# Moving weight decoding from a feed forward into the attention before it, two more PSUM banks at the start, and a later set of first splits

## The chip, the cores and the metric

The kernel runs on one core of a Trainium2 chip. The metric is the device time of one execution in microseconds (us). A measured change is compared with the kernel before on the same chip.

## The reference

```python
scores = scale * np.matmul(q, k.transpose(0, 1, 3, 2))      # 4 batches, 12 heads, 448 x 64
scores = np.einsum('bhij,hg->bgij', scores, w_pre)          # heads mixed
attn = softmax(scores)
attn = np.einsum('bhij,hg->bgij', attn, w_post)             # heads mixed again
x = np.matmul(attn, v)                                      # -> 1792 tokens x 768
h = x @ w_in                                                # 768 x 2048
x = (h / (1 + np.exp(-1.702 * h))) @ w_out                  # 2048 x 768
# then a mixture of 8 experts, one per token by argmax(x @ w_gate):
out[mask] = gate_w * eom * (np.maximum(x[mask] @ w1[e], 0) @ w2[e])
```

Everything is computed to float32 accuracy. `w_in` and `w_out` arrive as 64-bit floats.

## The kernel before

The program has three parts, each an unrolled list of instructions in an order written out by hand. Each engine runs its own instructions strictly in that order, and so does SP, which issues nearly all transfers.

**The attention** (`attention`) has 92 steps `s`, each of up to 20 query rows for all heads: four batches of 23 steps, in tiles of 120 rows. Scores are made by `qk` for a tile `t` of 112 queries (four to a batch) and one of six pairs of heads `p`, emptied from PSUM by `qk_ev` (one half on ScalarE, L166, one on VectorE, L167) into `so`, and sent to a DRAM tensor `S`. `relay(s)`, issued three steps ahead, reads them back as `G`, with heads on partitions. In step s TensorE does `premix(s)` (L184), VectorE the row maximum (L188), ScalarE the exponential (L191); `weights(s-1)` makes reciprocals on VectorE (L194, L195) and from them on GpSimd the matrices `M` (L198); `post(s-2)` multiplies by them (L207); `av` multiplies by V (L225). Before the loop stands an outset: scores of the first two tiles from unsplit q and k (`raw=True`), 12 pairs, two PSUM banks each, of which the pool `pq` has two.

**Split operands.** A float32 operand of later matmuls is split in a rounded part (a cast on ScalarE) and a rest (a subtraction on VectorE or GpSimd); three matmuls make one product. `split_w` (L317, L318) does so for a half of the feed forward's weights, `split_x` (L309, L310) for a chunk of its input.

**Decoding** (`Words`). The 32 halves of `w_in` and `w_out`, 128 x 768 each, come as 64-bit words. One half is decoded by four instructions on VectorE (L72 to L75) and an Abs on ScalarE (L67). The first NE halves are decoded one instruction at a time during the attention, in every other step from step 10 on, and lie in `pre`; the others are decoded in the first batch of the feed forward by `upto`, into `res`. `pre` also has two raw buffers behind the decoded halves.

**The feed forward** (`moe1`) has 64 steps, 16 for each of four batches: `l1` (18 matmuls, L326), tanh and product (`act`, L331, L332), split of the result (`act2`, L335, L336), `l2` (18 matmuls, L343). Its beginning is laid into the last steps of the attention: from step 88 on each step asks twice for the next of `EARLY`'s items. An item (t, kind, arguments) runs once the t-th request has been made; 'x' is `split_x`, 'w' `split_w`, 'l' `l1`, 't' `act`, 'u' `act2`; 'v' puts the subtraction on VectorE, 'p' on GpSimd.

**The experts** (`moe2`) follow. Their weights come through a ring of NR + NP buffers, NP in `pre`, NR in `res`; gathered tokens lie in `pre` behind the first NP.

Of the kernel before, what the change touches and what calls it, by code (L numbers as in the profile page):

```python
# [6 lines left out]
F32 = mybir.dt.float32  # L7
# [9 lines left out]
B, H, S, D = 4, 12, 448, 64  # L17

TI, TQ = 120, 112
TILES = [(i, min(TI, S - i)) for i in range(0, S, TI)]  # L20
DM, FF, E = 768, 2048, 8
# [3 lines left out]
CHUNK = {256: 128, 288: 96, 318: 106}  # L25
CM, CP, SL = max(CAP), 96, 1920

NE, NR, NP = 9, 12, 3

EARLY = [(2,'x',(2,'p')),(2,'x',(0,'v')),(3,'w',(0,0,'p')),(3,'x',(1,'v')),(4,'x',(5,'p')),(4,'x',(4,'v')),(5,'x',(3,'p')),  # L30
    (5,'w',(1,0,'p')),(6,'l',(0,)),(7,'w',(0,1,'v')),(8,'l',(1,)),(9,'w',(2,0,'p')),(9,'t',(0,)),(10,'u',(0,)),(11,'l',(2,)),(12,'w',(1,1,'v'))]
BIG = 2.0 ** 20


# [59 lines left out]
                    if k==2: self.after(i)  # L94
            self.nd=h[-1]+1

def attention(tc, qT, kT, vT, w_pre, w_post, x_out, words, beside=None):


    nc=tc.nc  # L100
    tiles=[(b,i0,n) for b in range(B) for i0,n in TILES]; NB=S//TQ
# [26 lines left out]
            sel(out=y,in_=y,pattern=[[0,12],[12,5]],compare_op=ALU.is_ge,fill=0.0,base=11,channel_multiplier=-1)  # L128
    R={}; K={}; V={}; Q={}; St={}; G={}; PM={}; E={}; ST={}; M2={}; PA={}; AT={}; PV={}; QP={}; WA={}; ready=set(); moved=set()
    def dma_k(b,p,n=2):  # L130
        if p%2==0: R['k',b,p//2]=wf.tile([128,2,S],F32,tag="kr",bufs=3,name="kr")
        nc.sync.dma_start(out=R['k',b,p//2][:,p%2:p%2+n],in_=kT[b,2*p:2*p+2*n].rearrange("(p h) d s -> (h d) p s",h=2))
    def split(k,d,x,shape,bufs,n=None):

# [17 lines left out]
        nc.sync.dma_start(out=R['q',t][:,lo:hi],in_=qT[b,:,6*TQ*j+lo:6*TQ*j+hi])  # L152
    def qk(t,p,raw=False):
        b=t//NB; i=slice(p*TQ,p*TQ+TQ)
        for z in range(2): QP[t,p,z]=pq.tile([TQ,S],F32,tag="q",name="psq")
        if raw: pairs=((R['q',t],R['k',b,p//2]),)
        else: (qh,ql),(kh,kl)=Q[t,],K[b,p//2]; pairs=((qh,kh),(qh,kl),(ql,kh))
        for x,(q,k) in enumerate(pairs):
            for z in range(2):
                r=slice(64*z,64*z+64)  # L160
                nc.tensor.matmul(QP[t,p,z],q[r,i],k[r,p%2],start=x==0,stop=x==len(pairs)-1)  # L161
# [8 lines left out]
    def relay(s):  # L170
        t,k,n=steps[s]; b,i0,_=tiles[t]; k+=i0
        if (b*NB+(k+n-1)//TQ,5) not in moved: raise RuntimeError('relay before scores')
        G[s]=w.tile([124,2,S],F32,tag="G",bufs=6,name="G")
        x=St[b].rearrange("i h j -> (i h) j")
        for a in units(s):
            if qs(s,a,1)==5: nc.sync.dma_start(out=G[s][64*a:64*a+60],in_=x[12*(k+10*a):12*(k+10*a)+120].rearrange("(c p) j -> p c j",c=2))
            else:
                for c in range(2): nc.sync.dma_start(out=G[s][64*a:64*a+12*qs(s,a,c),c],in_=x[12*(k+10*a+5*c):12*(k+10*a+5*c+qs(s,a,c))])
# [46 lines left out]
            for z in range(2): nc.tensor.matmul(ps[64*z:64*z+64,p%3,:n],V[b,2*p+z][:,j,:],AT[t][:,j,2*p+z,:n],start=j==0,stop=j==3)  # L225
    def av_ev(t,p):
        if p%3<2: return
        b,i0,n=tiles[t]; x=w.tile([128,3*TI],F32,tag="X",bufs=3,name="X")[:,:3*n]
        nc.vector.tensor_copy(x.rearrange("d (p i) -> d p i",p=3),PV.pop((t,p//3))[:,:,:n])  # L229
        nc.sync.dma_start(out=x_out[b,:,6*i0+(p-2)*n:6*i0+(p+1)*n],in_=x)  # L230
    from collections import defaultdict
    at={k:defaultdict(list) for k in 'qakvdKD'}
# [8 lines left out]
    for t in range(NT):  # L241
        b=tiles[t][0]
        m=first[t+2]-first[t+1] if t+1<NT else 3
        for p in range(6): at['a'][first[t+1]+2+p*m//6].append((t,p))
        if t%4==0:
            for h in (0,3,6,9): at['v'][first[t]+(h//3 if t==0 else (0,4,5,7)[h//3])].append((b,h))

    dma_q(0,(0,2*TQ)); dma_k(0,0,1); dma_k(0,1,1); dma_q(0,(2*TQ,6*TQ)); dma_k(0,2); dma_k(0,4)
    dma_q(1)
# [6 lines left out]
    for s in range(0,NS+6):  # L256
        on=s<NS
        if s+LEAD<NS: relay(s+LEAD)
        for x in at['d'][s]: dma_q(*x)
        for x in at['k'][s]: dma_k(*x)  # L260
        for x in at['v'][s]: dma_v(*x)
        if on:
            premix(s)
            for a in units(s): maxi(s,a); exp(s,a)
        if 0<=s-2<NS:
            for a in units(s-2): post(s-2,a)
            for c in range(2): post_ev(s-2,c)
        if 0<=s-1<NS: weights(s-1)
        for x in at['a'][s]: av(*x); av_ev(*x)
        if words is not None and s>7 and s%2==0 and next(words,"end")=="end": words=None  # L270
        for x in at['q'][s]: qk(*x)
        for x in at['q'][s]: qk_ev(*x)
        for x in at['K'][s]: split_k(*x)
        for x in at['D'][s]: split_q(*x)
        if s+LEAD>=NS-1 and beside is not None:
            if front is not None: front.close(); front=None
            for _ in range(2):
                if beside is not None and beside()=="end": beside=None
# [5 lines left out]
def moe1(tc, env, x_in, D, wg):  # L284

    nc=env.nc; NF=FF//128
    with ExitStack() as ctx, ExitStack() as late:
# [110 lines left out]
        at=0; did=set()  # L398
# [14 lines left out]
        for s in range(NS):  # L413
            b,f=steps[s]
            if s+1<NS and ('t',s+1) not in did: act(s+1)
            if s+2<NS and ('w',s+2,0) not in did: split_w(s+2,0)
            if b>0 and f==0: evac(b-1)
            if s+1<NS and ('u',s+1) not in did: act2(s+1)
            if s+1<NS and ('w',s+1,1) not in did: split_w(s+1,1)

            D.upto(NE+7*(s+1)//4)
            if b==3 and f>8:
                for i in range((f-9)*2,(f-8)*2 if f<NF-1 else NR+NP): env.load_w(i)
            nb_=b+1
            if s+2<NS and ('l',s+2) not in did: l1(s+2)
            if nb_<4 and f==NF-3:
                if b==0: split_w(16,0); did.add(('w',16,0))
                for c in range(6): split_x(nb_,c)
            if s==14: split_g()
            if b==0 and f<13: env.setup[f]()  # L430
            if f==3 and b<3: load_x(b+1)
            if b>0 and f in QS: route(b-1,(0,1,2,4,3)[QS.index(f)])
            if b==3 and f==8: rank(0)
            if b==3 and f==9: first(0)
            if b>0 and f in RS: i=RS.index(f); rows(b-1,i//2,i%2)
            if b>0 and f==1:
                def between(i):
                    if i==0: lsplit(b-1,0)
                    if i<5: lsplit(b-1,i+1)
                    lmm(b-1,i)  # L440
                l2(s,between)
            elif b>0 and f==2: l2(s,lambda i: lfin(b-1) if i==1 else None)
            elif s==NS-1:

                def between(i):
                    if i>0: evac(3,((2,3,4,5,0,1)[i-1],))
                    do(LR[i])
                def do(a):
                    for x in a:
                        if x[0]=='L': logits(3,(2,3,4,5,0,1)[x[1]],x[1]==0,x[1]==5)  # L450
                        elif x[0]=='R': route(3,x[1])
                        elif x[0]=='F': first(x[1])
                        else: rows(3,x[1],x[2])
                l2(s,between)
                between(6)
                do(LR[7])
            else: l2(s)
# [196 lines left out]
def moe2(tc, env, out):  # L654

    nc=env.nc
    with ExitStack() as ctx:
# [12 lines left out]
        def load_x(e):  # L670
            C,CP,NC=CS[e]
            if e==0: ID[e],ig=env.id0,env.ig0
            else:
                ID[e]=p.tile([128,3,4],I32,tag="id",bufs=3,name="id")[:CP,:NC,:]
                i=nc.sync.dma_start(out=ID[e],in_=env.ids[0:E*SL,:].rearrange("(e s) o -> e s o",e=E)[bass.ds(env.expert(e),1),0:C,:].rearrange("x (c p) o -> (x p) c o",p=CP))
                env.after(i.ins,'a')
                ig=p.tile([128,3],I32,tag="ig",bufs=2,name="ig")[:CP,:NC]
                nc.vector.tensor_scalar_min(ig,ID[e][:,:,0],float(NTOK-1))
            IG[e]=ig
            XS[e]=env.pre[:,(7+3*(e%2))*DM:(10+3*(e%2))*DM].rearrange("p (c n) -> p c n",c=3)[:CP,:NC,:]  # L680
            for c in range(NC):
                nc.gpsimd.indirect_dma_start(out=XS[e][:,c,:],out_offset=None,in_=env.rows,in_offset=IOA(ap=ig[:,c:c+1],axis=0))
        def load_g(e):
# [152 lines left out]
def moe_kernel(tc, qT, kT, vT, w_pre, w_post, w_in, w_out, wg, wm, out):  # L836
    with ExitStack() as ctx:
        x=ctx.enter_context(tc.tile_pool(name="xd",bufs=1,space=bass.MemoryType.DRAM)).tile([B,128,6*S],F32,name="x_dram")
        with tc.manual_schedule():
            pre=ctx.enter_context(tc.tile_pool(name="pre",bufs=1)).tile([128,(NE+4)*DM],F32,name="pre")  # L840
            D=Words(tc.nc,pre,w_in,w_out)
            def rest():
                env=make_env(tc,ctx,tc.nc); env.wm=wm; env.pre=pre
                yield from moe1(tc,env,x,D,wg)
                yield env
            g=rest()
            attention(tc,qT,kT,vT,w_pre,w_post,x,D.early(),lambda: next(g))
            env=None
            while not isinstance(env,Env): env=next(g)
            moe2(tc,env,out)  # L850
            env.stack.close()
        overflow(tc,env,out)
# [48 lines left out]
```

## Time and profile before

| | |
|---|---|
| median of 3 runs | 1306.34 us (1304.58 to 1307.55) |
| profiled execution | 1307.6 us, its span 1305.9 us |
| mean granted TensorE clock | 0.972 |
| TensorE busy | 1191.5 us (91%) |
| VectorE busy | 784.1 us (60%) |
| ScalarE busy | 613.4 us (47%) |
| GpSimd busy | 297.3 us (23%) |
| transfers | 201.12 MB |

Times in the profile run from the start of the span. PE is TensorE's matmuls, PEld its weight loads, DVE VectorE, ACT ScalarE, POOL GpSimd, SP the engine that issues transfers; L12 is line 12 of the kernel before. A busy share is an average over stages with different limits, so it is read stage by stage. "Idle before" is the time an engine stood still ahead of an instruction, with what ended it.

### The profile page before, as it was taken

The page shows a single profiled execution, that of the slowest core. Times are in us where ns is not written, and L with a number is a line of the kernel's source. Part 1 is how long each engine was busy: PE and PEld are TensorE (multiplying, and loading weights), DVE is VectorE, ACT ScalarE, POOL GpSimd, SP SyncE. Part 2 cuts the span into 40 slices and gives each one's busy share as a digit, 9 for nine tenths or more (in the row PEclk, how much of TensorE's full clock was granted, in tenths as well). Part 3 has the DMA queues.
Part 4 walks back from the last instruction along what each step waited for, and adds up shares of the span by engine and source line. Part 5 has one row for each costly group of instructions (what it writes and reads, how often), then busy time and mean ns, then how long its engine had stood idle before and what let it go on. Part 6 is the DMA issues. An engine that isn't in the chain of part 4 may idle for free. (4 is left out here: it accounts for less than half of the span.)

```text
span 1305.9 us, 32101 instructions
## 1 busy us (share of the span) xinstructions
PE 1191.5 (91%) x13254; PEld 1010.5 (77%) x13255; DVE 784.1 (60%) x1403; ACT 613.4 (47%) x1215; POOL 297.3 (23%) x366
## 2 busy tenths in 40 slices
PE   7788888889999888899999999999969799999996
PEld 2365656556666677788999899989969799999996
DVE  1576777667776499985435443545346555666662
ACT  2564665556555344444335433443325344444452
POOL 0442353344322400001211121112121230321110
PEclk9898999989989899999999999999989999999998
DMA  6897998888886146401000100001655754656400
GB/s 215 264 306 228 286 295 256 282 241 261 275 256 189 49 174 219 145 26 43 12 22 11 43 23 13 9 1 52 242 197 176 216 169 144 221 194 217 144 20 22
DMA packets 101715, 201.12 MB, mean 154 GB/s; under 512 B 30143, under 2 KB 72261, under 8 KB 101564
## 3 DMA queue, kind: packets, MB, share of 16 engines
q1 hardware_dynamic: 95484, 186.84, 45.5%
q0 software_dynamic: 6080, 12.18, 2.9%
q8 instruction: 106, 1.74, 0.6%
q14 instruction: 45, 0.37, 0.1%
HBM read 143.60 MB, written 56.43 MB: 153 GB/s over the span
## 5 line engine op out<-in xcount | busy, mean ns | idle before, releaser
L326 PE MATMUL psh<-x,ws 128*128 128x448 f32 x1152 | 250.9, 370 | 16.5 <-DVE ws L318 16.5
L343 PE MATMUL pso<-g,ws 128*128 128x448 f32 x1152 | 252.9, 370 | 0.0
L326 PEld LDWEIGHTS psh<-x,ws 128*128 128x128 f32 x1152 | 216.7, 189 | 40.6 <-DVE ws L318 20.2
L343 PEld LDWEIGHTS pso<-g,ws 128*128 128x128 f32 x1152 | 213.6, 188 | 20.3
L207 PEld LDWEIGHTS psa<-M,E 60*64 60x64 f32 x5760 | 107.5, 138 | 93.9 <-issue 51.8
L191 ACT ACTIVATE E<-psm,st 124x448 f32<-124x448 f32 x180 | 112.5, 630 | 101.9 <-DVE st L188 101.8
L318 DVE TENSOR_TENSOR ws<-res,ws 128x768 fp32r<-128x768 f32 x92 | 99.9, 1086 | 90.1 <-ACT ws L317 86.8
L198 POOL TENSOR_SCALAR M<-wq,st 124x60 f32<-124x60 f32 x180 | 99.8, 571 | 237.0 <-DVE st L195 226.6
L702 PE MATMUL psh<-xt,ws 128*128 128x256 f32 (+2 forms) x1152 | 149.4, 290 | 3.4 <-DVE hh L706 3.4
L336 POOL TENSOR_TENSOR g<-th,g 128x448 fp32r<-128x448 f32 x49 | 56.6, 1155 | 420.2 <-ACT g L335 419.6
L207 PE MATMUL psa<-M,E 60*64 60x60 f32 x5760 | 113.8, 223 | 42.1 <-issue 30.6
L702 PEld LDWEIGHTS psh<-xt,ws 128*128 128x128 f32 x1152 | 146.4, 191 | 4.2 <-DVE hh L706 4.0
L188 DVE TENSOR_REDUCE st<-psm 124x1 f32<-124x448 f32 x180 | 104.2, 618 | 30.9 <-PE psm L184 30.4
L669 DVE TENSOR_TENSOR ws<-res,ws 128x768 fp32r<-128x768 f32 x98 | 93.5, 959 | 30.1 <-ACT ws L668 27.0
L721 PE MATMUL psy<-ws,hh 128*128 128x384 f32 x576 | 110.9, 346 | 0.0
L335 ACT CAST g<-th 128x448 fp32r<-128x448 f32 x64 | 36.3, 567 | 144.0 <-PE pso L343 102.6
L721 PEld LDWEIGHTS psy<-ws,hh 128*128 128x128 f32 x576 | 101.4, 191 | 0.0
L184 PE MATMUL psm<-G,wp 60*64 60x448 f32 x720 | 97.5, 585 | 2.2 <-DMA G<-S 1.4
L167 DVE TENSOR_SCALAR so<-psq 112x448 f32<-112x448 f32 x96 | 59.8, 623 | 61.8 <-PE psq L161 54.5
L225 PE MATMUL psv<-AT,V 128*64 128x120 f32 (+1 forms) x1536 | 95.3, 269 | 0.5 <-DVE X L229 0.5
L215 DVE COPY AT<-psa 128x480 f32<-128x480 f32 (+1 forms) x92 | 61.6, 670 | 41.9 <-PE psa L207 41.5
L166 ACT ACTIVATE so<-psq 112x448 f32<-112x448 f32 x96 | 52.2, 543 | 69.1 <-PE psq L161 45.4
(190 smaller groups left out, 1513.0 us busy)
## 6 DMA issues: line engine op xcount, KB each, us to landing
S<-so SPq DMA_DIRECT2D x96, 392.0 KB
G<-S SPq DMA_DIRECT2D x176, 210.0 KB
res<-in_wm SPq DMA_DIRECT2D x43, 768.0 KB
pre<-in_wm SPq DMA_DIRECT2D x13, 768.0 KB
pre<-in_w_in SPq DMA_DIRECT2D x11, 768.0 KB
pre<-in_w_out SPq DMA_DIRECT2D x11, 768.0 KB
V<-in_vT SPq DMA_DIRECT2D x16, 384.0 KB
qr<-in_qT SPq DMA_DIRECT2D x15, 336.0 KB
```

Of the source, the lines that this page charges most:

```text
L184: nc.tensor.matmul(PM[s,a][64*c:64*c+64],wp[r],G[s][r,c,:],start=True,stop=True)
L188: nc.vector.reduce_max(ST[s][:,0,a:a+1],PM[s,a][:124],axis=AX.X,negate=True)
L191: nc.scalar.activation(E[s,a],PM.pop((s,a))[:124],AF.Exp,bias=ST[s][:,0,a:a+1],scale=1.0,accum_out=ST[s][:,1,a:a+1])
L198: nc.gpsimd.tensor_scalar_mul(M2[s,a],wq,st[:,3,a:a+1])
L207: nc.tensor.matmul(PA[s][64*cp:64*cp+64,c,240*a+60*cc:240*a+60*cc+60],e[r,j:j+64],m[r],start=True,stop=True)
L225: for z in range(2): nc.tensor.matmul(ps[64*z:64*z+64,p%3,:n],V[b,2*p+z][:,j,:],AT[t][:,j,2*p+z,:n],start=j==0,stop=j==3)
L318: (e or nc.vector).tensor_tensor(out=t[:,1,:],in0=r,in1=t[:,0,:].bitcast(F32),op=ALU.subtract)
L326: nc.tensor.matmul(ps[:,:TB],t[:,wz,c],x[:,xz,:],start=k==0,stop=k==17); k+=1
L343: nc.tensor.matmul(OB[b][o][:,:TB],t[:,wz,c],g[:,xz,:],start=f==0 and k==0,stop=f==NF-1 and k==2)
L669: nc.vector.tensor_tensor(out=t[:,1,:],in0=r[:,c],in1=t[:,0,:].bitcast(F32),op=ALU.subtract)
L702: nc.tensor.matmul(ps,w[:,a,k*128:(k+1)*128],x[:,b,:],start=k==0 and (a,b)==(0,0),stop=k==5 and a==1)
L721: nc.tensor.matmul(PY[e][2*c+z],h[:,a,c*CP:c*CP+CP],w[:,b,z*384:z*384+384],start=f==0 and k==0,stop=f==7 and k==2)
```

## The change

Seven edits come together.

- NE goes from 9 to 13, NR from 12 to 10, NP from 3 to 5: four more halves are decoded during the attention and kept in `pre`, `res` is two rows shorter, and the ring of the experts keeps its 15 buffers. The places in `pre` follow.
- Decoding in the attention starts one step later and advances in two steps of three. In the feed forward it advances by 7 halves in 5 steps, where it was 7 in 4.
- The raw K of the first batch lies in the free end of `pre` (`spare`). `kr` has two buffers for three, `G` five for six, `X` two for three.
- Raw scores of every odd pair of heads take their two banks from `pm`, the pool of `premix`, which has three.
- The four loads of V of the first batch are issued in steps 3 to 6, where it was 0 to 3.
- EARLY's items run two requests, one step, later.
- All of EARLY's splits are on VectorE; six were on GpSimd.

```diff
-NE, NR, NP = 9, 12, 3
-
-EARLY = [(2,'x',(2,'p')),(2,'x',(0,'v')),(3,'w',(0,0,'p')),(3,'x',(1,'v')),(4,'x',(5,'p')),(4,'x',(4,'v')),(5,'x',(3,'p')),
-    (5,'w',(1,0,'p')),(6,'l',(0,)),(7,'w',(0,1,'v')),(8,'l',(1,)),(9,'w',(2,0,'p')),(9,'t',(0,)),(10,'u',(0,)),(11,'l',(2,)),(12,'w',(1,1,'v'))]
+NE, NR, NP = 13, 10, 5
+
+EARLY = [(4,'x',(2,'v')),(4,'x',(0,'v')),(5,'w',(0,0,'v')),(5,'x',(1,'v')),(6,'x',(5,'v')),(6,'x',(4,'v')),(7,'x',(3,'v')),
+    (7,'w',(1,0,'v')),(8,'l',(0,)),(9,'w',(0,1,'v')),(10,'l',(1,)),(11,'w',(2,0,'v')),(11,'t',(0,)),(12,'u',(0,)),(13,'l',(2,)),(14,'w',(1,1,'v'))]
...
     def dma_k(b,p,n=2):
-        if p%2==0: R['k',b,p//2]=wf.tile([128,2,S],F32,tag="kr",bufs=3,name="kr")
+
+        if p%2==0: R['k',b,p//2]=spare[:,p*S:p*S+2*S].rearrange("d (p j) -> d p j",p=2) if b==0 else wf.tile([128,2,S],F32,tag="kr",bufs=2,name="kr")
...
     def qk(t,p,raw=False):
-        for z in range(2): QP[t,p,z]=pq.tile([TQ,S],F32,tag="q",name="psq")
+
+        for z in range(2): QP[t,p,z]=pm.tile([128,S],F32,tag="m",name="psq")[:TQ] if raw and p%2 else pq.tile([TQ,S],F32,tag="q",name="psq")
...
     def relay(s):
-        G[s]=w.tile([124,2,S],F32,tag="G",bufs=6,name="G")
+        G[s]=w.tile([124,2,S],F32,tag="G",bufs=5,name="G")
...
     def av_ev(t,p):
-        b,i0,n=tiles[t]; x=w.tile([128,3*TI],F32,tag="X",bufs=3,name="X")[:,:3*n]
+        b,i0,n=tiles[t]; x=w.tile([128,3*TI],F32,tag="X",bufs=2,name="X")[:,:3*n]
...
-            for h in (0,3,6,9): at['v'][first[t]+(h//3 if t==0 else (0,4,5,7)[h//3])].append((b,h))
+            for h in (0,3,6,9): at['v'][first[t]+(3+h//3 if t==0 else (0,4,5,7)[h//3])].append((b,h))
...
-        if words is not None and s>7 and s%2==0 and next(words,"end")=="end": words=None
+        if words is not None and s>7 and s%3<2 and next(words,"end")=="end": words=None
...
-            D.upto(NE+7*(s+1)//4)
+            D.upto(NE+7*(s+1)//5)
...
-            XS[e]=env.pre[:,(7+3*(e%2))*DM:(10+3*(e%2))*DM]
+            XS[e]=env.pre[:,(2*NP+1+3*(e%2))*DM:(2*NP+4+3*(e%2))*DM]
...
-            attention(tc,qT,kT,vT,w_pre,w_post,x,D.early(),lambda: next(g))
+            attention(tc,qT,kT,vT,w_pre,w_post,x,D.early(),pre[:,NE*DM:],lambda: next(g))
```

## Rows read from the trace of the kernel before

**Rows 1.** Busy time by stretch: PE, PEld, DVE, ACT, POOL, granted clock, DMA share, GB/s.

```profile
460.00:576.00 116.00, 99.49 (x466) 87.71 (x465) 109.60 (x146) 54.45 (x82) 0.60 (x3) 0.99 0.46 157
576.00:700.00 124.00, 124.00 (x624) 112.39 (x624) 61.83 (x96) 53.51 (x94) 22.09 (x19) 1.00 0.09 23
50.00:430.00 380.00, 333.75 (x8166) 231.42 (x8158) 274.95 (x599) 224.41 (x539) 138.28 (x197) 0.97 0.85 262
```

**Rows 2.** Groups by line, 460 to 575 us: busy us, mean ns | idle before, releaser.

```profile
L326 PEld LDWEIGHTS psh<-x,ws 128*128 128x128 f32 x234 | 44.4, 193 | 24.3 <-DVE ws L318 20.2 <-ACT ws L317 0.4
L318 DVE TENSOR_TENSOR ws<-res,ws 128x768 fp32r<-128x768 f32 x22 | 21.0, 956 | 0.5
L75 DVE SCALAR_TENSOR_TENSOR res<-wa,res 128x768 f32<-128x768 f32 x22 | 20.2, 954 | 0.4
...
L336 DVE TENSOR_TENSOR g<-th,g 128x448 fp32r<-128x448 f32 x13 | 8.1, 622 | 4.9 <-ACT g L335 4.9
...
L72 DVE TENSOR_SCALAR res<-res 128x768 int32<-128x768 int32 x10 | 5.5, 554 | 0.0
```

**Rows 3.** Timeline of PE from 576 us: start us, us, what.

```profile
577.84 3.90 PE L326 MATMUL psh<-x,ws 128*128 128x448 f32 x18
...
592.52 3.81 PE L326 MATMUL psh<-x,ws 128*128 128x448 f32 x18
```

**Rows 4.** Timeline at the end of the attention, 404 to 478 us.

```profile
427.70 3.33 DVE L310 TENSOR_TENSOR x<-xs,x 128x448 fp32r<-128x448 f32 x2 [4.50 <-ACT x L309]
...
428.48 2.08 POOL L318 TENSOR_TENSOR ws<-pre,ws 128x768 fp32r<-128x768 f32 x1
...
433.65 1.83 PEld L207 LDWEIGHTS psa<-M,E 60*64 60x64 f32 x64 [6.71 <-POOL M L198]
...
457.36 3.98 PE L343 MATMUL pso<-g,ws 128*128 128x448 f32 x18
```

**Rows 5.** Timeline at the outset, 0 to 46 us.

```profile
6.75 1.84 PE L161 MATMUL psq<-kr,qr 64*112 64x448 f32 x4 [0.72 <-DVE so L167]
...
9.21 1.96 PE L161 MATMUL psq<-kr,qr 64*112 64x448 f32 x4 [0.63 <-ACT so L166]
...
31.29 0.62 DVE L167 TENSOR_SCALAR so<-psq 112x448 f32<-112x448 f32 x1 [3.81 <-DMA S<-so]
...
33.89 0.62 DVE L167 TENSOR_SCALAR so<-psq 112x448 f32<-112x448 f32 x1 [1.98 <-PE psq L161]
...
44.73 0.51 DVE L139 CAST Qh<-qr 128x672 fp32r<-128x672 f32 x1 [5.44 <-DMA qr<-in_qT]
```

**Rows 6.** Timeline of POOL, steps with and without a decode.

```profile
90.91 1.36 POOL L198 TENSOR_SCALAR M<-wq,st 124x60 f32<-124x60 f32 x2 [2.45 <-DVE st L195]
94.68 0.83 POOL L198 TENSOR_SCALAR M<-wq,st 124x60 f32<-124x60 f32 x2 [2.42 <-DVE st L195]
```

**Rows 7.** Waits, 82 to 396 us: us in total, times, longest.

```profile
PE psa L207 <- issue: 26.7, 18, 3.5
PEld psa L207 <- POOL M L198: 24.6, 49, 2.2
```

**Rows 8.** Queues, transfer sizes; two stretches of 25 us, and PE's waits in one.

```profile
q8 instruction: 106, 1.74, 0.6%
...
S<-so SPq DMA_DIRECT2D x96, 392.0 KB
...
pre<-in_w_in SPq DMA_DIRECT2D x11, 768.0 KB
...
250.00:275.00 25.00, 16.80 (x430) 12.08 (x432) 13.36 (x31) 12.53 (x29) 8.64 (x10) 0.98 1.00 320
...
325.00:350.00 25.00, 24.37 (x600) 17.78 (x592) 19.26 (x44) 14.89 (x37) 8.04 (x12) 1.00 0.86 264
...
PE psa L207 <- issue: 8.8, 3, 3.5
```

**Rows 9.** Busy time by stretch at the outset.

```profile
4.00:8.00 4.00, 3.09 (x8) 0.94 (x8) 0.62 (x1) 0.54 (x1) 0.00 (x0) 1.00 0.97 303
```

More of the change, by code (lines that the diff above doesn't have):

```diff
@@ L95, in upto, with attention @@
             self.nd=h[-1]+1
-def attention(tc, qT, kT, vT, w_pre, w_post, x_out, words, beside=None):
+def attention(tc, qT, kT, vT, w_pre, w_post, x_out, words, spare, beside=None):
     nc=tc.nc
@@ L679, in load_x @@
             IG[e]=ig
-            XS[e]=env.pre[:,(7+3*(e%2))*DM:(10+3*(e%2))*DM].rearrange("p (c n) -> p c n",c=3)[:CP,:NC,:]
+            XS[e]=env.pre[:,(2*NP+1+3*(e%2))*DM:(2*NP+4+3*(e%2))*DM].rearrange("p (c n) -> p c n",c=3)[:CP,:NC,:]
             for c in range(NC):
```

## The prediction, made before the result was known

> **What bounds the kernel now.** I read the table of busy time over stretches first, because the average over the span mixes stages with different limits. Three stretches matter [rows 1]. In the attention (50 to 430 us) TensorE is busy 334 of 380 us, VectorE 275, and the transfers take 0.85 of their engines: nothing is full, and everything waits a little for everything. In the first batch of the first feed forward (460 to 576) VectorE is busy 109.6 of 116 us and TensorE 99.5. From 576 TensorE is busy without a gap, so whatever an earlier stage saves reaches the end one for one.
>
> The groups by line, inside 460 to 575, say what the feed forward waits for [rows 2]: TensorE's weight loads stood idle 24.3 us, 20.2 of them for the splits of L318, and L318 itself hardly waited (0.5 us). So VectorE sets the pace here, and much of its work is the decoding of L72 to L75. How fast TensorE could go shows right behind: with no decode left, two steps of 36 matmuls each go from 577.84 to 592.52 [rows 3], 7.34 us a step. From the first `l2` at 457.36 [rows 4] to 577.84 there are 13.5 such steps (that `l2`, then `l1` and `l2` of 13 steps): 99 us of work in 120.5 us. The stretch can give back 21 us at most.
>
> Last the timeline of the two places at which the diff puts things elsewhere. At the end of the attention VectorE stood at L310, waiting 4.50 us for a cast and then running two splits in 3.33 us while GpSimd did a split of its own; the row maxima had to come behind it, and TensorE's weight loads sat idle 6.71 us until 433.65 [rows 4]. At the outset one pair of score matmuls takes 1.84 us, then both banks must be emptied, and the next pair starts 2.46 us after it; the evictions of the second tile end in the same rhythm (31.29, 33.89), the first of these held up 3.81 us by a store [rows 5].
>
> **The change part by part**, against the profiled execution (span 1305.9, time 1307.6 us, 1.3 above the median of the runs).
>
> *Four halves leave the feed forward.* 23 halves were decoded there, 19 remain. One half is one L72 (0.554 us) and three of L73 to L75 (0.954 us each) [rows 2]: 3.42 us, four of them 13.7 us. In the stretch VectorE is 0.945 busy [rows 1], so nearly all of it can show. Left are 19 x 3.42 + 14 x (two L318 at 0.956, the split of `g` at 0.622 and the tanh product, taken as long: 3.16) = 109 us by summed durations, against 123 before; scaled to the 120.5 us of the stretch, 107. TensorE needs 99, so the two become nearly equal, and as the decodes come by one or two halves a step, some of the unevenness will stay. I take -11, two short of that; ends -8 (unevenness costs 40 per cent) and -13.7 (all of it).
>
> *The same four halves enter the attention*, 16 instructions of VectorE more, two steps of three instead of one of two. (In steps 81 to 87 there were none.) VectorE has room, so the price is delay, not work: behind a two-input decode the two `M` products of GpSimd took 1.36 us, without 0.83 [rows 6], so TensorE's next `post` gets its operand 0.53 later. TensorE's loads waited for `M` 49 times in the 70 or so steps from 82 to 396 [rows 7], that is in 0.7 of them. 12 two-input decodes x 0.53 x 0.7 = 4.5, and 0.5 for the four others and for four more Abs on ScalarE (224 of 380 us busy [rows 1], so mostly covered): +5. Ends: 0 (steps without a decode take it back) and +15 (16 x 0.95, were VectorE on the chain throughout).
>
> What two engines do to each other here has a rule in the Trainium skill, "SBUF — State Buffer", section "SBUF: two separate sides": a VectorE instruction with two SBUF inputs and a GpSimd one exclude each other, and the later waits for the whole of the earlier. The trace agrees (0.53 is less than the 0.95 of a decode: it had begun before). What the rule allows at its worst, a decode that begins just ahead of each `M`, is among the rivals below.
>
> *Weights moved with them*: 4 x 768 KB [rows 8] = 3.1 MB more during the attention, some 10 us of the transfer engines at the 320 GB/s of the stretch from 250 to 275 [rows 8]. TensorE's "issue" idle at L207 was 8.8 us in that stretch (share 1.00), and it was busy 16.8 of 25 us there, but 24.4 in 325 to 350 (0.86) [rows 8]; TensorE's program itself comes by a queue of 106 packets, 1.74 MB [rows 8], so I read these waits as instructions arriving late, an inference. 10 us of full transfer engines are 0.4 such stretches: 0.4 x 8.8 = 3.5 at worst; nearer the middle, +1.7, ends 0 and +5. The Trainium skill, "Runtime: NRT & Kernel Launch", section "Instruction fetch mechanics", calls the cost of a block boundary mostly hidden. By that this term would be 0 and the sum 1.7 less; the 8.8 us speak against it.
>
> *The tail.* The splits of EARLY come one step later and all on VectorE. The wait for the cast (4.50 us [rows 4]) goes, because the transfer has landed by then, and so does the doubling of durations: splits of `x` without a GpSimd split beside them should take what that of `g`, of the same shape, takes (0.62 [rows 2]). The first stall of 6 us shrinks to perhaps 0.5. Late next are `post` and the first `l1`, one step later and so no longer a filler in front of `post(90)`: an estimate from the order of the work, 1.5 us of new idle time there. -6 + 0.5 + 1.5 = -4; ends -1 and -6.
>
> *The outset.* With two more banks TensorE need not wait for the eviction: 1.84 for 2.46, 0.62 x 5 gaps = -3.1 in the first tile. The second hangs on stores and on three buffers of `so`: VectorE waited 3.81 us for a store [rows 5]. That chain moves up by the same 3.1, and its last two gaps shrink to 1.84 too: -1.2. Sum -4.3. Ends: -1 (the transfer engines are at 0.97 from 4 to 8 us [rows 9], so that the stores, not the banks, may limit) and -7 (gaps at 1.3, what a store of 392 KB [rows 8] takes at the 303 GB/s of that row: 7 gaps x 1.15 = 8, less one for the loads that still run).
>
> *Moved and shortened.* The four loads of V leave steps 0 to 3, where the first `Qh` waited 5.44 us for its transfer [rows 5], and go to steps 3 to 6, among the stores and G loads: 0, ends -1.5 and +2 (one load is 1.3 us at the same rate). With two buffers of `kr` the third K load of a batch now waits on SP for `split_k` of the next step, and stores and G loads queue behind it for about a step (380 us are some 91 steps, 4.2 each [rows 1]). G is loaded three steps ahead, which hides it: +0.5, ends 0 and +4. G with five buffers and X with two: nothing, since four G live at once and an X is sent a tile (six steps) before its buffer returns. NR, NP and the place of `XS` shift names; halves lie under the same turn of `load_w`: 0.
>
> Sum: -11 + 5 + 1.7 - 4 - 4.3 + 0 + 0.5 = -12.1 on 1307.6, or 1295.5; less the 1.3 that the profile lies above the median, 1294.2. I say **1294**.
>
> **Rivals.**
> *The attention hides the decodes* (0 instead of +5) and the outset gives its 7: 1294 - 5 - 2.7 = 1286. For it: VectorE is idle 28% there. Against: 49 waits for `M`.
> *GpSimd held for whole decodes, and TensorE soon the bound*: were each of the 12 two-input decodes to hold `M` for its full 0.95 us, they would cost 11, and the feed forward gives 8: 1294 + 6 + 3 = 1303, hardly to be told from now. The rule quoted from the Trainium skill ("SBUF — State Buffer", the same section) would allow it. For it: 49 waits of 70; against: 1.36 is what a pair took behind a decode.
> *Slower*: full transfer engines starve TensorE's program. The issue waits of L207, 26.7 us from 82 to 396 [rows 7], are worst where the share is 1.00, and the change adds bytes there and moves the loop up against the same bytes. Were they to grow by 20 us (1.3 us in each of fifteen stretches of 25 us), 1294 - 1.7 + 20 = 1312. From 14 us on, the gain is gone. Against: only 3% more bytes (3.1 MB on 262 GB/s x 380 us [rows 1], 100 MB).
> *The banks do nothing*, since the stores limit: 4.3 less gain, 1298; that is inside the forecast's own range.
>
> **How the numbers follow.** What this kernel's measurement can tell from no change is 0.2%, 2.6 us: faster is below 1303.7, slower above 1309. Forecast 0.62 (1289 to 1300 by its own ends), hidden 0.14, held 0.12, slower 0.12. Of the forecast and the first rival all is faster (0.76), of the held rival a third (0.04), the rest of it mostly the same: faster 0.80, same 0.08, slower 0.12. The range leaves out the slower rival and half of the hidden one's low side: 1284 to 1305.
>
> **What would show it.** Right: between the first `l2` and the first gapless stretch some 109.5 us instead of 120.5, with VectorE still above 0.9; the first `l2` about 1 us earlier than 457.36; L310 near 0.6 us, no idle of 6 us at L207 in the tail; pairs at the outset under 2 us apart, and a first `Qh` near 40. Wrong: an attention longer by more than 5 us once outset and tail are taken out, more issue idle at L207, or SP waiting for a K split while TensorE waits for G. The prediction fails most easily in the attention, where a price of 5 is set between 0 and 15.

## The result, and the profile after

The changed kernel takes 1312.67 us (median of 20 runs, 1302.84 to 1323.79), the kernel before 1306.51 (20 runs). The ratio is 1.0059 (95% interval 1.0040 to 1.0078): slower by 0.6%, 7.7 us, where 1294 was forecast. The two medians by themselves are 6.2 us apart; the ratio leaves out the longest run of the changed kernel, a slow one, and the text goes by it. The profiled execution took 1314.0 us, span 1312.3, mean granted clock 0.959 (0.972 before).

Line numbers are those of each run's own kernel: L168, L169 and L209 of the changed one are L166, L167 and L207 of the kernel before.

The stages first, from four marks in the timeline of each trace: the first cast to `Qh`, the last `premix`, the first `l2`, the first `l1` of the second batch.

| us | to first `Qh` | attention | tail | feed forward, first batch | rest |
|---|---|---|---|---|---|
| before | 44.73 | 382.02 | 30.61 | 120.48 | 728.1 |
| after | 38.73 | 399.16 | 29.59 | 120.47 | 724.3 |

The outset gained 6.0 us, the attention lost 17.1. The feed forward, at which the largest term was aimed, did not move.

Busy time by stretch after (columns as in [rows 1]); the first row is the feed forward's first batch, the second the attention:

```profile
467.00:588.00 121.00, 107.26 (x503) 95.99 (x498) 103.51 (x137) 53.89 (x81) 3.07 (x22) 0.94 0.38 126
...
50.00:430.00 380.00, 328.59 (x7759) 227.49 (x7754) 278.81 (x591) 216.69 (x518) 138.41 (x187) 0.95 0.83 261
```

And the same stretch of the feed forward in the kernel before:

```profile
457.00:578.00 121.00, 104.49 (x499) 92.08 (x495) 113.30 (x152) 57.06 (x85) 3.08 (x22) 0.99 0.45 152
```

VectorE does 9.8 us less in the feed forward (103.5 for 113.3; its term said 13.7), and yet the 121 us stay. TensorE's idle time fell by 2.8 us only (16.5 to 13.7), and its matmuls took 2.8 longer (104.5 to 107.3) at a lower granted clock (0.94 for 0.99). In the attention TensorE does less in the same 380 us (328.6 for 333.8), with the transfers no fuller.

What SP waited for in the attention of the changed kernel, 40 to 430 us (us in total, times, longest), and then what the engines waited for, 46 to 420 us, columns as in [rows 7]:

```profile
SPq L170 <- DVE so L169: 80.2, 53, 7.3
...
SPq L133 <- POOL Kl L141: 23.0, 3, 9.2
```

```profile
PE psa L209 <- issue: 23.0, 17, 3.0
...
ACT so L168 <- DMA S<-so: 19.0, 5, 9.5
...
DVE so L169 <- DMA S<-so: 17.7, 4, 8.8
PEld psq L163 <- ACT so L168: 14.9, 9, 5.9
```

L133 is the K load, L141 the split that frees its buffer: three waits of 23.0 us in all, one for each later batch; in the kernel before, that wait is 0.4 us. The evictions of scores then waited 19.0 and 17.7 us for score stores to empty a `so`, and TensorE for the evictions. The kernel before has a single row of that kind in the same stretch:

```profile
ACT so L166 <- DMA S<-so: 2.3, 2, 1.2
```

The `issue` wait of the slower rival is not larger than before (30.6 us there in the same stretch).

The outset after, VectorE's timeline, answers to [rows 5]:

```profile
18.94 0.62 DVE L169 TENSOR_SCALAR so<-psq 112x448 f32<-112x448 f32 x1 [0.76 <-DMA S<-so]
27.84 0.62 DVE L169 TENSOR_SCALAR so<-psq 112x448 f32<-112x448 f32 x1 [8.27 <-DMA S<-so]
28.77 0.63 DVE L169 TENSOR_SCALAR so<-psq 112x448 f32<-112x448 f32 x1 [0.31 <-DMA S<-so]
30.29 0.62 DVE L169 TENSOR_SCALAR so<-psq 112x448 f32<-112x448 f32 x1 [0.89 <-PE psq L163]
...
38.73 0.51 DVE L140 CAST Qh<-qr 128x672 fp32r<-128x672 f32 x1 [5.59 <-DMA qr<-in_qT]
```

The tail after, VectorE's and the weight loads' timelines, answers to [rows 4]:

```profile
440.52 1.16 DVE L312 TENSOR_TENSOR x<-xs,x 128x448 fp32r<-128x448 f32 x2 [1.91 <-ACT x L311]
```

```profile
438.87 1.27 PEld L209 LDWEIGHTS psa<-M,E 60*64 60x64 f32 x64 [0.79 <-POOL M L200]
...
445.27 1.80 PEld L209 LDWEIGHTS psa<-M,E 60*64 60x64 f32 x64 [4.25 <-POOL M L200]
```

The stall of 6.71 us is down to 0.79, and one of 4.25 stands a `post` later.

### The profile page after: what moved, and what is told of

It reads as the page before. It is cut to its first block, busy times and chain, and to the rows that moved or that the text cites. A ratio compares the mean times of both kernels' runs of the same rounds, so it can differ in the third digit from the quotient of the medians.

```text
span 1312.3 us, 32112 instructions
## 1 busy us (share of the span) xinstructions
PE 1195.2 (91%) x13254; PEld 1018.6 (78%) x13255; DVE 788.0 (60%) x1409; ACT 612.9 (47%) x1215; POOL 295.6 (23%) x360
## 3 DMA queue, kind: packets, MB, share of 16 engines
q8 instruction: 106, 1.74, 0.6%
## 5 line engine op out<-in xcount | busy, mean ns | idle before, releaser
L328 PE MATMUL psh<-x,ws 128*128 128x448 f32 x1152 | 254.2, 374 | 13.7 <-DVE ws L320 12.5
L328 PEld LDWEIGHTS psh<-x,ws 128*128 128x128 f32 x1152 | 220.7, 192 | 37.1 <-DVE ws L320 14.8
L209 PEld LDWEIGHTS psa<-M,E 60*64 60x64 f32 x5760 | 110.5, 142 | 88.8 <-issue 44.8
L200 POOL TENSOR_SCALAR M<-wq,st 124x60 f32<-124x60 f32 x180 | 105.7, 603 | 249.2 <-DVE st L197 237.7
L209 PE MATMUL psa<-M,E 60*64 60x60 f32 x5760 | 118.0, 228 | 34.6 <-issue 23.0
L320 DVE TENSOR_TENSOR ws<-res,ws 128x768 fp32r<-128x768 f32 x76 | 82.7, 1088 | 76.8 <-ACT ws L319 73.3
L186 PE MATMUL psm<-G,wp 60*64 60x448 f32 x720 | 102.1, 600 | 1.1 <-DMA G<-S 0.8
L169 DVE TENSOR_SCALAR so<-psq 112x448 f32<-112x448 f32 x96 | 59.7, 622 | 69.1 <-PE psq L163 33.8
L227 PE MATMUL psv<-AT,V 128*64 128x120 f32 (+1 forms) x1536 | 98.2, 274 | 2.0 <-issue 1.4
L671 DVE TENSOR_TENSOR ws<-res,ws 128x768 fp32r<-128x768 f32 x80 | 76.3, 959 | 24.3 <-ACT ws L670 21.7
L168 ACT ACTIVATE so<-psq 112x448 f32<-112x448 f32 x96 | 52.1, 543 | 79.1 <-DMA S<-so 31.5
L227 PEld LDWEIGHTS psv<-AT,V 128*64 128x64 f32 x1536 | 78.4, 142 | 8.8 <-issue 2.3
```

The costliest lines, as they stand in the source:

```text
L186: nc.tensor.matmul(PM[s,a][64*c:64*c+64],wp[r],G[s][r,c,:],start=True,stop=True)
L200: nc.gpsimd.tensor_scalar_mul(M2[s,a],wq,st[:,3,a:a+1])
L209: nc.tensor.matmul(PA[s][64*cp:64*cp+64,c,240*a+60*cc:240*a+60*cc+60],e[r,j:j+64],m[r],start=True,stop=True)
L320: (e or nc.vector).tensor_tensor(out=t[:,1,:],in0=r,in1=t[:,0,:].bitcast(F32),op=ALU.subtract)
L328: nc.tensor.matmul(ps[:,:TB],t[:,wz,c],x[:,xz,:],start=k==0,stop=k==17); k+=1
L671: nc.vector.tensor_tensor(out=t[:,1,:],in0=r[:,c],in1=t[:,0,:].bitcast(F32),op=ALU.subtract)
```

## The experiments

Two theories of the loss were set against each other. *K wait*: SP issues strictly in order, so a K load that waits for its buffer holds everything behind it. *Decodes*: the four halves, with their weights and the fuller transfers, slow the attention. For the feed forward: VectorE's work is less but comes in bunches, against the rival that something else sets the pace of a step.

**The third K load, three steps later.** It is then due after the split of the first has freed its buffer; nothing else is undone.

```diff
-            for p in (0,2,4): at['k'][z-11+p].append((b,p)); ...
+            for p in (0,2,4): at['k'][z-11+p+(3 if p==4 else 0)].append((b,p)); ...
```

> The changed kernel, with the third K load of a batch issued three steps later (step z-4 for z-7), behind the split that frees its buffer. Theory 1 (in the changed kernel SP stands 23 us at these loads, the score stores queue behind them, evictions find no buffer): SP no longer waits there, the attention loses some 13 us of the 17 it had gained over the kernel before, and the whole takes about 1299 us (ratio 0.994). Rival (the sixteen decodes and 3.1 MB more transfers are what lengthens the attention): within 3 us of the changed kernel, about 1311 (1.004).

1301.83 us, ratio to before 0.9915 (0.9881 to 0.9948), so the changed kernel is 1.45% above it (1.0059/0.9915). Its waits of the engines, 50 to 430 us:

```profile
DVE so L169 <- DMA S<-so: 4.2, 3, 2.1
...
ACT so L168 <- DMA S<-so: 3.5, 2, 2.0
```

SP has no row with `Kl` any more, the waits of the evictions fell from 36.7 to 7.7 us (2.3 in the kernel before), and the attention from 399.2 to 388.3. One line turns the loss into a gain, with thirteen halves still decoded there.

**Two K buffers alone**, in the kernel before.

```diff
-        if p%2==0: R['k',b,p//2]=wf.tile([128,2,S],F32,tag="kr",bufs=3,name="kr")
+        if p%2==0: R['k',b,p//2]=spare[:,p*S:p*S+2*S]... if b==0 else wf.tile([128,2,S],F32,tag="kr",bufs=2,name="kr")
```

> The kernel before, with one thing of the change: two buffers for raw K (the first batch's lies in the free end of pre). Theory 1: SP waits for the K split in three places, 20 us or more in all, and the whole takes about 1318 us (1.009). Rival (SP's wait is hidden by the three steps of lead, the decodes cost): 1306 to 1308 (1.000).

1317.88 us, 1.0064 (1.0042 to 1.0087). This edit by itself makes the kernel before as slow as the whole change does. SP's waits, 40 to 430 us:

```profile
SPq L132 <- POOL Kl L140: 24.8, 3, 10.7
```

**Decodes dealt evenly in the feed forward**: after each step 5.6 instructions of decoding rather than one or two halves of four; the rest as changed.

```diff
-            D.upto(NE+7*(s+1)//5)
+            D.fine(4*NE+28*(s+1)//5)      # decode(i,k) one by one, k = 0..3
```

> The changed kernel, with the decodes of the feed forward dealt out by single instructions (5.6 a step) in place of one or two whole halves a step. Theory 2 (the four halves less on VectorE gave nothing because a step of two halves still stalls TensorE and one of a single half leaves VectorE idle): the stretch from the first l2 to the first l1 of the second batch falls from 120.5 to about 108 us, the whole to about 1302 (0.997). Rival (the chain through ScalarE and the product of tanh sets the pace of a step, however the decodes lie): 118 or more, the whole about 1311 (1.003).

1309.61 us, 1.0015 (0.9988 to 1.0043). The feed forward's first batch took 113.7 us rather than 120.5: -6.8 in the place it was made for, -0.4% against the changed kernel.

**Both edits together.**

> The changed kernel with both edits, the third K load later and the decodes dealt out evenly. Theories 1 and 2 together: about 1288 us (0.986). If only the first holds 1299, if only the second 1301, if neither 1311.

1298.64 us, 0.9903 (0.9870 to 0.9936). The whole time doesn't tell it from the K load alone (0.9915), though the feed forward again took 113.6 us in its trace.

Those two answers opened the second set: the parts alone.

**The banks alone**, in the kernel before.

```diff
-        for z in range(2): QP[t,p,z]=pq.tile([TQ,S],F32,tag="q",name="psq")
+        for z in range(2): QP[t,p,z]=pm.tile([128,S],F32,tag="m",name="psq")[:TQ] if raw and p%2 else pq.tile([TQ,S],F32,tag="q",name="psq")
```

> The kernel before with one part of the change: raw scores of odd pairs of heads in two banks of pm. Theory 3 (the outset's gain is real and carried to the end): the first Qh near 39 us (44.7 before) and the whole 5 to 6 us shorter, about 1302 (0.996). Rival (the transfers are what the first 100 us wait for, so the gain is lost by step 12): the first Qh near 39, the whole within 2 us of the kernel before.

1299.65 us, 0.9943 (0.9920 to 0.9966): 7.4 us. First `Qh` at 37.52, 7.2 earlier.

**The new EARLY alone**, in the kernel before (the list of the change's diff).

> The kernel before with one part of the change: the new EARLY (all first splits on VectorE, a step later). Theory 4 (the wait for the cast only moves one step on, as in the changed kernel): from the last premix to the first l2 30 us as before, the whole within 2 us (0.999). Rival, the step of the prediction: 26 us there, the whole 4 us shorter (0.997).

1303.58 us, 0.9977 (0.9953 to 1.0002): 3 us, not quite told from nothing. The tail took 27.5 us in its trace, 3.1 less than in the kernel before, which is nearer to the step of the prediction (26) than to 30.

**Nine halves in the attention** as before, on top of the later K load; all else as changed.

```diff
-NE, NR, NP = 13, 10, 5
+NE, NR, NP = 9, 12, 3
...
-        if words is not None and s>7 and s%3<2 and next(words,"end")=="end": words=None
+        if words is not None and s>7 and s%2==0 and next(words,"end")=="end": words=None
...
-            D.upto(NE+7*(s+1)//5)
+            D.upto(NE+7*(s+1)//4)
```

> The changed kernel with the third K load later, and with the move of the four halves undone (nine decoded in the attention in every other step, 7 in 4 steps of the feed forward; banks, V, EARLY, K and the shorter pools as changed). Theory 5 (the move costs the attention 5 to 7 us and, dealt out in whole halves, gives the feed forward nothing): shorter than the same kernel with the thirteen halves by 5 to 7 us, about 0.986 of the kernel before. Rival (VectorE hides the decodes in the attention): the same within 2 us, 0.991.

1297.49 us, 0.9926 (0.9899 to 0.9952), against 0.9915 with thirteen: moving the four halves bought and cost nothing that the time can tell. The 5 to 7 us that I expected did not come: the attentions of the two traces are 387.3 and 388.3 us.

**The tail's loads earlier**: `x` is loaded four steps sooner and EARLY's items keep their steps, on the kernel with both edits.

```diff
-        if s+LEAD>=NS-1 and beside is not None:
+        if s+LEAD>=NS-5 and beside is not None:      # and 8 more requests on every item of EARLY
```

> The kernel with the third K load later and the decodes dealt out evenly, in which the beginning of the feed forward is opened four steps earlier and each item of EARLY keeps its step: only the load of x runs ahead. Theory 4 (VectorE stands at the first split of x because that load lands late): L312's wait for the cast goes, the last premix to the first l2 falls from 30 to some 26 us, the whole 3 to 4 us shorter, 0.987. Rival (the splits themselves, ahead of the last row maxima on VectorE, are the delay): 29 us or more, 0.990.

1298.44 us, 0.9932 (0.9906 to 0.9958), no better than 0.9903 without. In its trace the wait at the first split of `x` is 0.64 us (1.94 without), the idle ahead of the second `post` 3.19 (4.27), the tail 27.6 (29.8). But the even decodes and V first, which load `x` no earlier than the change does, show the same 0.64 and tails of 28.7 and 28.6, so these two traces don't show that the earlier load did it.

**Banks and EARLY only**, in the kernel before, asks whether anything else of the change earns; two more kernels ask whether the K wait's price holds in other company.

> The kernel before with two parts of the change, the banks at the outset and the new EARLY. Theory (parts add up): 0.9943 x 0.9977 = 0.992, as the whole change with the third K load later, so that nothing else in it brings time. Rival (the thirteen halves and the even dealing bring something on top): clearly above the 0.990 of the kernel with both edits, 0.995 or more.

1298.20 us, 0.9924 (0.9900 to 0.9948).

> The kernel before with the banks at the outset and two buffers for raw K. Two buffers alone cost 0.64%, and in the changed kernel undoing their wait gave 1.4%. If the earlier loop makes the wait dearer, 1.006 or more; if the two only add up, 0.9943 x 1.0064 = 1.0007.

1312.97 us, 1.0027 (1.0003 to 1.0051): the two K buffers cost 0.84% beside the banks (1.0027/0.9943), with SP 28.7 us in three waits. The plain sum that I expected, 1.0007, lies inside the interval, and 1.006 outside.

> The changed kernel with the move of the four halves undone and the third K load left where the change has it. Against the kernel with nine halves and the later load (0.9926) it prices the K wait without the four halves, against the changed kernel (1.0059) the four halves under the wait. If the halves make the wait dearer, 1.000 (0.0064 of wait added); if not, 1.006.

This is the kernel with nine halves and the K load back in its old step: 1310.86 us, 1.0022 (0.9995 to 1.0048), 0.97% above the one without the wait. Here too the interval takes in one of the two values expected, 1.000, and not 1.006.

**V first again**: both edits, and the loads of V back in steps 0 to 3.

```diff
-            for h in (0,3,6,9): at['v'][first[t]+(3+h//3 if t==0 else (0,4,5,7)[h//3])].append((b,h))
+            for h in (0,3,6,9): at['v'][first[t]+(h//3 if t==0 else (0,4,5,7)[h//3])].append((b,h))
```

> The kernel with the third K load later and the decodes dealt out evenly, with the V loads of the first batch back in steps 0 to 3. If V among the stores of steps 3 to 6 costs, 1 to 3 us shorter (0.989); if V in step 0 delays the first q, 1 us longer (0.992); no difference: 0.990 to 0.991.

1294.53 us, 0.9889 (0.9842 to 0.9936), the lowest of all, but not to be told from 0.9903 with V later or from 0.9924 of banks and EARLY.

The stages of the traces, sorted by the two things in dispute (one trace each):

| attention, us | with the K wait | without |
|---|---|---|
| 13 halves | 399.2 (after), 396.9 (even decodes): mean 398.0 | 388.3 (later K), 384.4 (both), 384.5 (tail loads), 383.6 (V first): mean 385.2 |
| 9 halves | 390.1 (two K buffers), 393.4 (with banks), 392.1 (nine, K wait): mean 391.9 | 382.0 (before), 376.0 (banks), 373.9 (EARLY), 380.3 (both), 387.3 (nine): mean 379.9 |

Down a column the halves make 5 to 6 us (385.2 - 379.9, 398.0 - 391.9); across a row the K wait makes 12 to 13 (5 to 17 in the five pairs that differ by the wait alone). Single cells of a kind lie up to 13 us apart, so the means carry this, and the times of the pairs beside them. One sign sorts the traces without overlap: the evictions waited 30 to 49 us for score stores (50 to 420 us) in the five with the K wait, and 0 to 9 in the nine without.

## Why the prediction failed

The forecast was -12.1 us, the measurement +7.7. Two terms hold nearly all of the difference: the K wait was put 12 us too low, and the feed forward was to give 11 that did not come.

**The step that failed: "G is loaded three steps ahead, which hides it: +0.5, ends 0 and +4".** The wait on SP was foreseen. Its length was put at about a step, 4.2 us; it was 7.7 on average (23.0 in three). The price was 12 to 13 us of the traces, and +0.64% (two K buffers alone) to +1.45% (changed kernel against later K load) of the times, 8 to 19 us, in five pairs of kernels (between them 0.84, 0.97 and 1.13%). The intervals of the first and the last do not meet (0.42 to 0.87, about 1.1 to 1.8), but by the medians these two are 0.60 and 1.1%; that the wait costs more in the company of the other edits is not shown. The cover that I named holds for the loads of G alone: TensorE waited 4.9 us for them in the changed kernel, 4.7 before (46 to 420 us). The score stores stand in the same queue, and they have no lead: `so` has three buffers. The first event, SP's timeline after:

```profile
53.59 1.47 SPq L178 DMA_DIRECT2D G<-S  x2
61.37 0.41 SPq L133 DMA_DIRECT2D kr<-in_kT  x1
61.82 0.68 SPq L148 DMA_DIRECT2D V<-in_vT  x1
62.61 0.36 SPq L170 DMA_DIRECT2D S<-so  x1
```

GpSimd's, the split that it waited for:

```profile
59.24 2.10 POOL L141 TENSOR_TENSOR Kl<-kr,Kh 128x896 fp32r<-128x896 f32 x1 [0.70 <-ACT Kh L139]
```

ScalarE's evictions, and TensorE's matmuls, in the same stretch:

```profile
54.66 0.56 ACT L168 ACTIVATE so<-psq 112x448 f32<-112x448 f32 x1
...
57.78 0.56 ACT L168 ACTIVATE so<-psq 112x448 f32<-112x448 f32 x1
...
61.80 0.54 ACT L168 ACTIVATE so<-psq 112x448 f32<-112x448 f32 x1
67.75 0.54 ACT L168 ACTIVATE so<-psq 112x448 f32<-112x448 f32 x1 [5.40 <-DMA S<-so]
```

```profile
68.34 0.79 PE L163 MATMUL psq<-Kh,Qh 64*112 64x448 f32 x2 [2.16 <-ACT so L168]
```

SP issues nothing from 55.06 to 61.37, when `Kl` is done. The store of the scores evicted at 54.66 leaves only at 62.61. The evictions at 57.78 and 61.80 fill the other two buffers; the next waits 5.40 us for that store to land, and TensorE, in order too, 2.16 us for the eviction. SP waits so once for each later batch. So the stall came not where the list of signs put it (TensorE waiting for G) but at `so`. The later K load removes SP's wait and all but 7.7 of the evictions' 36.7 us, and the two buffers alone bring both (24.8 and 30.4 us); the cause is shown from both sides.

The Trainium skill, "Perfetto Trace Analysis", section "DMA Optimizations", says that it may make sense to give inputs to one issuing engine and outputs to another, "to allow more dynamic spread". The trace shows a case for it, 23.0 us of a load's wait ahead of stores; no run here tried it, since a later load was enough.

**"Four halves leave the feed forward": -11 forecast, 0 measured.** The work left (9.8 us of VectorE, 13.7 said) and the bound did not. The failing thought was "nearly all of it can show": an engine that works in order cannot bank idle time. TensorE's timeline around a step with two halves, after:

```profile
509.31 0.57 PE L328 MATMUL psh<-x,ws 128*128 128x448 f32 x2
512.12 4.93 PE L328 MATMUL psh<-x,ws 128*128 128x448 f32 x16 [2.24 <-DVE ws L320]
```

and VectorE's, through that step and the one with one half behind it:

```profile
503.55 0.96 DVE L320 TENSOR_TENSOR ws<-pre,ws 128x768 fp32r<-128x768 f32 x1
...
508.85 1.82 DVE L75 SCALAR_TENSOR_TENSOR res<-wa,res 128x768 f32<-128x768 f32 x2
...
511.12 0.95 DVE L320 TENSOR_TENSOR ws<-res,ws 128x768 fp32r<-128x768 f32 x1
...
512.61 0.96 DVE L320 TENSOR_TENSOR ws<-res,ws 128x768 fp32r<-128x768 f32 x1
...
517.66 0.62 DVE L334 SCALAR_TENSOR_TENSOR th<-th,psh 128x448 f32<-128x448 f32 x1 [0.58 <-ACT th L333]
...
521.33 0.63 DVE L338 TENSOR_TENSOR g<-th,g 128x448 fp32r<-128x448 f32 x1 [1.99 <-ACT g L337]
```

From 504.43 to 510.67 VectorE works through eight decode instructions without a gap, and the split TensorE waits for comes behind them, at 511.12. In the next step VectorE is through early and stands still for `th` and `g`: the tanh and the cast that ScalarE makes ahead of them wait in turn for TensorE's matmuls. The groups after, 468 to 587 us, show both sides, columns as in [rows 2]:

```profile
L328 PEld LDWEIGHTS psh<-x,ws 128*128 128x128 f32 x234 | 48.0, 208 | 21.0 <-DVE ws L320 14.8 <-ACT ws L319 2.0
...
L338 DVE TENSOR_TENSOR g<-th,g 128x448 fp32r<-128x448 f32 x14 | 8.7, 622 | 10.8 <-ACT g L337 10.8
```

The weight loads' idle time fell from 24.3 to 21.0, VectorE's own before `g` rose from 4.9 to 10.8. Dealt evenly, the same work gives this (both edits, busy time by stretch, and TensorE's timeline):

```profile
453.00:567.00 114.00, 104.45 (x494) 92.91 (x489) 104.52 (x136) 53.79 (x81) 3.08 (x22) 0.97 0.41 134
```

```profile
511.90 3.51 PE L336 MATMUL psh<-x,ws 128*128 128x448 f32 x16 [1.39 <-DVE ws L328]
```

TensorE's idle time is 9.6 us of 114, and the 16 matmuls shown take 3.51 us rather than 4.93. So the uneven dealing took 7 of the 11: the first batch took 111.8 to 113.7 us in all four traces with even dealing, 120.1 to 122.2 in the ten others, with nine halves and with thirteen. The rest: TensorE's work in the stretch is 104.5 us, where I had 99 from the step of 7.34, although [rows 1] had 99.5 us of it in 116 of the 120.5 already.

**The decodes in the attention, +5, and their weights, +1.7:** 5 to 6 us by the means of the table, near the 6.7 forecast together. By times, thirteen halves against nine are -0.1% without the K wait, not told from nothing, and +0.4% with it, barely told. The price per `M` can be seen: from 82 to 396 us GpSimd took 583 to 606 ns for one in the eight traces with nine halves, 624 to 637 in the six with thirteen. The Trainium skill's rule of exclusive access ("SBUF — State Buffer", "SBUF: two separate sides") agrees in kind; no run tells it from other effects of the decodes. But TensorE's loads did not wait longer for `M`: 24.6 us before, 24.9 after, 23.6 with the later K load, in 49, 43 and 44 waits. The step of the prediction, a `post` later by 0.53 in 0.7 of the steps, is not seen, so the near size is no proof of it; through what the halves lengthen the attention stays open, and so does the share of their transfers.

**The outset, -4.3:** the mechanism was right, the size 6.0 here and 7.2 alone. The sixth eviction of VectorE, the last of the first tile, comes 4.9 us earlier (14.13 for 19.03), not 3.1, and the wait for a store ahead of the tenth took part of that back (8.27 us for 3.81): the tenth comes 3.45 earlier (27.84 for 31.29), so that its nearness to the -3.1 is in part luck. The two gaps behind it, put at 1.84 each, were 0.93 and 1.52, because with four banks those scores were ready while the store was waited for. The rival that banks do nothing is out.

**The tail, -4:** the first stall shrank as said and L312 takes 0.62 us an instruction, but "the transfer has landed by then" failed in this trace (1.91 us of wait at 440.52; it was 0.64 in seven of the ten traces with the new list, 1.74 to 1.94 in three), and the new idle time ahead of the next `post` was 4.25 us (2.2 to 4.3 in the ten), not 1.5. Measured -1.0; over ten traces with the new list the tail is 28.0 us, over four with the old 30.7. With the new list it is 26.0 to 27.5 in the four traces with nine halves and 27.6 to 29.8 in the six with thirteen, so the list alone is worth some 3 us, and the moved halves seem to take part of it back; how is not shown.

**V, `G`, `X`, NR, NP at nothing:** as far as the runs can tell. Nine halves with the later K load carry the edits of V, `G` and `X`, thirteen with it those of NR and NP too, and both are as fast as banks and EARLY alone (0.9926, 0.9915 and 0.9924).

**The slower rival** had the sign and not the mechanism: the `issue` waits at `post` from 82 to 396 us were 20.6 us after, 26.7 before [rows 7]. That its 1312 is the time measured is luck.

With the measured sizes the sum is 12.4 for K, 5.7 for the decodes, 0, -6.0 and -1.0: +11.1, where the spans differ by 6.4 and the times by 7.7. The rest of the program was 3.7 us shorter in that one trace, and 728 to 732 in the thirteen others; what that is stays open. So what the change gains is its outset and its tail, some 0.8%, and one wait spends it.

## What to carry to other kernels

Before a transfer is allowed to wait on an in-order queue, list everything behind it and the slack of each; the cover is the shortest slack, here that of stores from three buffers, not that of loads three steps ahead. Work taken off an engine that stalls another shows only in the steps that stall: look at the longest step, not at the sum over a stretch, and deal the work evenly before moving it. An edit that makes room (a buffer less) deserves the same working as those that it makes room for.

## What the hardware showed that was not expected

A short stall of TensorE can cost more than its length. The 16 matmuls that took 4.93 us came behind 2.2 us in which TensorE was idle; those that took 3.51 came behind 1.4 us. Busy time by stretch of the two places, after and with both edits (columns as in [rows 1]):

```profile
509.90:512.10 2.20, 0.00 (x0) 0.00 (x0) 2.20 (x4) 0.82 (x2) 0.00 (x0) 0.94 0.95 388
512.10:517.00 4.90, 4.88 (x17) 4.42 (x18) 4.71 (x6) 1.31 (x2) 0.00 (x0) 0.68 0.31 128
```

```profile
511.90:515.30 3.40, 3.40 (x17) 3.16 (x18) 3.34 (x5) 1.28 (x2) 0.00 (x0) 1.00 0.53 217
```

The granted clock was 0.68 in the one, between the two levels of 1.2 and 2.4 GHz, and 1.00 in the other. The length of the stall does not decide it: in the changed kernel's own trace, one as long was followed by 16 matmuls at full pace.

```profile
556.58 3.50 PE L328 MATMUL psh<-x,ws 128*128 128x448 f32 x16 [2.23 <-DVE ws L320]
```

The first batch has 34 stalls of 1.9 to 2.3 us in the fourteen traces; behind 13 of them the next 16 matmuls took about 5 us, behind the 21 others 3.5. What decides is not shown. At the outset the four banks let TensorE finish early and then stand still, and the clock went down with it; after again:

```profile
20.00:24.00 4.00, 1.27 (x6) 0.33 (x2) 0.00 (x0) 0.00 (x0) 0.00 (x0) 0.97 0.91 221
24.00:28.00 4.00, 0.00 (x0) 0.00 (x0) 0.16 (x1) 0.18 (x1) 0.00 (x0) 0.50 1.00 344
28.00:44.00 16.00, 10.86 (x64) 3.72 (x68) 6.45 (x13) 7.08 (x15) 8.61 (x6) 0.50 0.77 228
```

With nothing to do from 24 to 28 us it was granted 0.50, that is 1.2 GHz, and 0.50 still from 28 to 44 us, at 10.86 us of work in 16. In the kernel before it was granted 1.00 until 40 us, and 0.50 only from 44 to 52.

One kernel's own runs spread more than I had assumed: 1302.8 to 1316.5 us for the changed one without its longest. Twenty runs of each tell 0.2% apart, one trace of a stage does not, and a difference of 4 us between two single traces is no evidence.
